# The later heads' exponentials stay in PSUM until their low halves are taken, and GpSimd makes the remainders of q and k in two column halves

## The chip, the cores and the metric

The kernel runs on one core of a Trainium2 chip. Five engines work side by side, each through its own queue in order: TensorE (PE; its weight loads are listed apart as PEld), VectorE (DVE), ScalarE (ACT), GpSimd (POOL) and SyncE (SP), which issues the transfers. The metric is the device time of one execution in microseconds. Before the change the median of three runs is 1068.91 us (1068.48 to 1070.02).

## The reference, cut to what matters

```python
# q, k, v: (8 batches, 8 heads, 576 rows, 64);  f: (8, 8, 576);  w_in: (512, 2048);  w_out: (2048, 512)
scores = q @ k.T / 8
cum    = cumsum(log(clip(f, 1e-4, 1)))
scores = where(causal, -1e9, scores + cum[:, None] - cum[None, :])
attn   = exp(scores - scores.max(-1))
attn   = attn / (attn.sum(-1) + 1e-9)
x      = (attn @ v), heads side by side              # 4608 x 512
h      = x @ w_in
g      = h * clip(h + 3, 0, 6) / 6
out    = g @ w_out
```

All of it is float32. Products on TensorE run on float16 pairs: a number is split into a high half (its cast to float16) and a low half (the number less its high half), and a product takes three matmuls (high by high, high by low, low by high). q and k are split likewise into a rounded part and a remainder.

## The kernel before, in words

Batch 0's heads run in another form: first two heads at a time for the first 256 rows (four steps "A", numbers 0 to 3), then each head for the rest (eight steps "B", 4 to 11). The other seven batches are the later batches: 56 steps "F", one for a head, numbers 12 to 67. A name such as `pn_40_1` is the tile `pn` of step 40, half 1.

A step F works in two halves. Half 0 holds the query chunks 1, 4 and 0 (192, 576 and 64 keys wide), half 1 the chunks 2 and 3 (320 and 448 wide), by `NAT`. For each half, in `rows`:

- PE makes the scores, row by row, into the two-bank PSUM tile `pn` (L611 from the rounded parts `TQ`, `TK`, L614 from the remainders in `T7`, `T1`). `pn` comes from the pool `ps_s`, which has two such tiles.
- DVE adds the causal mask `W`, copies the chunk into the SBUF tile `pp` and takes its row maximum (L622, followed by a small read of the accumulator). `pn` is then free for the next user. DVE makes the bias `nb` (L628).
- ACT takes the exponential in place in `pp` (L634) and casts it into the high half in a ring buffer `hl` (L648).
- The low halves are exponential less high half: the wide part of chunks 1 to 4 at L651, and the last 64 columns of two chunks in one instruction, 128 by 2 by 64, at L657 (the profile lists it as 128x128). Chunk 0's 64 columns are L662. `PL_POOL` and `B0_POOL` say which of these GpSimd does: in the eight heads of batch 1 (12 to 19) chunk 3's wide part, and in heads 20 to 67 all of L657 and L662. GpSimd zeroes a corner of `hl` first (L645).
- A transposing DMA turns `hl` into `pT`, from which PE makes the head's 40 matmuls of attention by v (`pav`, L694 to L699) one step later. DVE scales them (L730 to L732) and, after a head pair, splits them (ACT L737, DVE L738) for `xT`.

GpSimd rounds q and k (`parts`, L449 and L450) two steps ahead, and makes the remainders one step ahead (`rests`, L458 and L461, one instruction of 64 x 576 each).

The dense layers run in units between the attention's pieces. `h_unit` makes 128 columns of h for up to 512 rows (twelve matmuls, L777 to L779, into `ph`; ACT L783, DVE L786, ACT L787, DVE L788), and `out_unit` makes 128 rows of the output (48 matmuls, L824 to L826, into `po`; then ACT L830). `ph` and `po` rotate over three PSUM tiles once batch 0's first units are done. Before `out_unit` can run, `w_out` has to be scaled and split: ACT L284 makes a high half, DVE L295 the low half, sixteen pieces, all of them in the stretch around heads 12 to 18. A unit of a batch can only start when the batch's heads are done.

The order on each engine is not that of the code: the kernel is built with a scheduler that plays the program through its own model of time and writes each engine's queue accordingly. What a tile waits for, who holds it, and how long the planner takes an instruction to be, decide which row comes next.

Of the kernel before, what the change touches and what calls it, by code (L numbers as in the profile page):

```python
# [11 lines left out]
F32 = mybir.dt.float32  # L12
# [3 lines left out]
ALU = mybir.AluOpType  # L16
# [4 lines left out]
def kernel(  # L21
# [10 lines left out]
    nc = tc.nc  # L32

    NHEAD, D, S = qk.shape
# [5 lines left out]
    P = 128  # L40
# [13 lines left out]
    p2 = ctx.enter_context(tc.tile_pool(name="p2", bufs=2))  # L54
# [19 lines left out]
    W = cpool.tile([P, 4 * P + P], BF16, name="W")  # L74
# [23 lines left out]
    NV = len(VH)  # L98
    NRING = 3
    NSP = 3  # L100
    PL_POOL = ((3, ), ())
    NAT = ((1, 4, 0), (2, 3))
    B0_POOL = ((0, 0), (1, 1))
    W_AHEAD = (4, 5)
    W_ORDER = 0
    POOL_REST = ((0, 0, 0, 0), (0, 0, 0, 0))
# [1 line left out]
    TQ = [cpool.tile([97, SP], F32R, name=f"TQ{i}") for i in range(NQK)]  # L108
    TK = [cpool.tile([97, SP], F32R, name=f"TK{i}") for i in range(NQK)]
    T1 = [cpool.tile([P, SP], F32R, name=f"T1{i}") for i in range(NL)]  # L110
# [333 lines left out]
    def parts(v):  # L444
# [4 lines left out]
        nc.gpsimd.tensor_scalar(TK[i][0:D, 0:nk], s[D:, 0:nk], **one)  # L449
        nc.gpsimd.tensor_scalar(TQ[i][0:D, 0:nq], s[0:D, q0:q0 + nq], **one)  # L450

    def rests(v):
        i, j = v % NQK, v % NL
        s = ST[v % NST]
        nq, nk, q0 = spans(v)
        nc.sync.dma_start(T7[j].bitcast(F32)[0:D, 0:nq], TQ[i].bitcast(F32)[0:D, 0:nq])
        nc.sync.dma_start(T1[j].bitcast(F32)[D:, 0:nk], TK[i].bitcast(F32)[0:D, 0:nk])
        nc.gpsimd.tensor_tensor(  # L458
            T7[j][D:, 0:nq], s[0:D, q0:q0 + nq], TQ[i][0:D, 0:nq].bitcast(F32), op=ALU.subtract
        )  # L460
        nc.gpsimd.tensor_tensor(  # L461
            T1[j][0:D, 0:nk], s[D:, 0:nk], T1[j][D:, 0:nk].bitcast(F32), op=ALU.subtract
        )


    def chunks(v):
# [119 lines left out]
    o = 0  # L586
    for half in NAT:
        for c in half:
            HT[c] = o
            o += (2 * c + 1) * P  # L590
    PLACE = {1: 0, 4: 192, 0: 768, 3: 0, 2: 512}
    ringh = [t.bitcast(F16) for t in ring]

    def rows(v):
# [7 lines left out]
        for half in range(2):  # L602
            pn = ps_s.tile([P, 1024], F32, tag="S", name=f"pn_{v}_{half}")
            hl = ringh[(2 * v + half) % NRING]
            for c in NAT[half]:
# [3 lines left out]
                for a, e in zip(cut, cut[1:]):  # L609
# [4 lines left out]
                    nc.tensor.matmul(  # L614
                        dst, T7[j][:, qs], T1[j][:, a:e], start=False, stop=True
                    )
            pp = p2.tile([P, 832], F32, tag="Pp", name=f"pp_{v}_{half}")
            at, w = {}, 0
            for x, c in enumerate(NAT[half]):
                o, r, kw = PLACE[c], RR[c], RB[c] + RR[c]  # L620
                at[c] = w
                nc.vector.tensor_tensor_reduce(  # L622
                    pp[:r, w:w + kw], pn[:r, o:o + kw], W[:r, 4 * P + r - kw:4 * P + r],
                    1.0, -3.0e38, ALU.add, ALU.max, accum_out=mc[:r, e0 + x:e0 + x + 1],
                )
                w += kw
            e1 = e0 + len(NAT[half])
            nc.vector.tensor_scalar(  # L628
                nb[:, e0:e1], mc[:, e0:e1], -0.125, math.log(PSC), op0=ALU.mult, op1=ALU.add
# [435 lines left out]
```

## Time and profile before

| | |
|---|---|
| median of three runs | 1068.91 us |
| the profiled execution's own time | 1069.33 us |
| its span (first to last instruction of the trace) | 1067.5 us |
| mean granted TensorE clock | 0.988 |
| busy: PE, DVE, ACT, POOL | 1006.3, 731.1, 587.3, 403.4 us |

The span and the execution's time differ by 1.8 us, which no instruction of the trace covers. PE's busy time is the union of modelled durations: matmuls are pipelined, one of 512 columns is listed with 0.38 us while the next starts about 0.22 us behind it, so a matmul with nothing behind it still counts in full. Views by stretch matter here, since the stretches have different limits.

### The profile page before, as it was taken

What the parts mean: (1) busy time and instruction counts of PE and PEld (TensorE: products, weight loads), DVE (VectorE), ACT (ScalarE), POOL (GpSimd) and SP (SyncE); (2) the same over time, 40 slices, a digit from 0 to 9 for tenths busy, and PEclk for the clock granted to TensorE, in tenths of its full rate; (3) what the DMA queues carried; (4) which work ended last, traced back from release to release, by engine and by line L of the source; (5) the groups of instructions that cost most, each with busy time, mean ns of one, the idle gap of its engine ahead of it and who ended that gap; (6) DMA issues with size and microseconds to landing.
All of it is one profiled execution on the core that took longest, in us unless ns stands there. A gap on an engine that the chain in (4) does not pass through costs nothing.

```text
span 1067.5 us, 21157 instructions
## 1 busy us (share of the span) xinstructions
PE 1006.3 (94%) x7650; PEld 598.0 (56%) x7650; DVE 731.1 (68%) x1887; ACT 587.3 (55%) x1189; POOL 403.4 (38%) x505
## 2 busy tenths in 40 slices
PE   2799977899999999999999999999999999999897
PEld 1577844665555755555555755555555755444543
DVE  6978899996876768866886668846895677105300
ACT  4778666764764557545654557635764566115301
POOL 8343466443443444344443444534443330000000
PEclk9989989999999999999999999999999999999999
DMA  8965647955856776667575766566557554010000
GB/s 240 308 187 194 151 109 145 220 114 118 169 116 134 139 153 124 113 148 165 118 134 118 158 140 119 118 136 167 119 112 145 103 100 74 12 40 1 1 20 30
DMA packets 259155, 133.78 MB, mean 125 GB/s; under 512 B 226948, under 2 KB 228540, under 8 KB 259052
## 3 DMA queue, kind: packets, MB, share of 16 engines
q1 hardware_dynamic: 259052, 132.44, 55.7%
q8 instruction: 60, 0.98, 0.4%
q14 instruction: 43, 0.35, 0.1%
HBM read 47.93 MB, written 9.73 MB: 54 GB/s over the span
## 4 chain that ended last, share of the span: by engine, by line
PE 76%; DVE 12%; ACT 5%; issue 4%; DMA 2%; POOL 1%; SPq 0%; DVEq 0%; ACTq 0%; POOLq 0%
PE po L824 9%; PE po L826 9%; PE po L825 9%; PE ph L777 9%; PE ph L778 9%; PE ph L779 9%; PE pn L611 3%; PE pn L614 3%; DVE pp L622 2%; DVE ring L651 2%; PE po_r L826 1%; PE pav L698 1%; ACT pp L634 1%; PE po_r L824 1%; PE po_r L825 1%
## 5 line engine op out<-in xcount | busy, mean ns | idle before, releaser
L634 ACT ACTIVATE pp<-pp,nb 128x192 f32<-128x192 f32 x280 | 138.6, 552 | 170.3 <-DVE nb L628 150.8
L777 PE MATMUL ph<-xT,w 128*128 128x512 f16 (+1 forms) x576 | 198.8, 357 | 2.5 <-DVE r L786 2.4
L825 PE MATMUL po<-w,gT 128*128 128x512 f16 x512 | 192.6, 382 | 8.0 <-DVE w L295 8.0
L779 PE MATMUL ph<-xT,w 128*128 128x512 f16 (+1 forms) x576 | 198.0, 356 | 0.0
L778 PE MATMUL ph<-xT,w 128*128 128x512 f16 (+1 forms) x576 | 197.8, 356 | 0.0
L651 DVE TENSOR_TENSOR ring<-pp,ring 128x128 f16<-128x128 f32 (+2 forms) x216 | 138.0, 650 | 85.6 <-ACT ring L648 84.7
L824 PE MATMUL po<-w,gT 128*128 128x512 f16 x512 | 190.4, 383 | 5.8 <-DVE r_r L813 2.7
L826 PE MATMUL po<-w,gT 128*128 128x512 f16 x512 | 192.4, 383 | 0.0
L622 DVE CUSTOM_DVE_ANT_0 pp<-pn,W 128x192 f32<-128x192 f32 x280 | 123.3, 482 | 29.3 <-PE pn L614 28.0
L461 POOL TENSOR_TENSOR T<-ST,T 64x576 fp32r<-64x576 f32 (+1 forms) x68 | 100.9, 1483 | 107.2 <-DMA T<-TK 85.8
L786 DVE SCALAR_TENSOR_TENSOR r<-r,ph 128x512 f32<-128x512 f32 (+1 forms) x144 | 89.1, 620 | 61.4 <-ACT r L783 60.6
L611 PE MATMUL pn<-TK,TQ 68*128 68x192 f32 x336 | 124.8, 385 | 3.8 <-issue 2.2
L788 DVE TENSOR_TENSOR gT<-r,gT 128x512 f16<-128x512 f32 (+1 forms) x144 | 111.6, 781 | 22.0 <-ACT gT L787 20.6
L614 PE MATMUL pn<-T,T 128*128 128x192 f32 x336 | 115.2, 368 | 0.2 <-POOL T L461 0.2
L783 ACT ACTIVATE r<-ph,bias_r,SC 128x512 f32<-128x512 f32 (+1 forms) x144 | 103.9, 725 | 19.2 <-PE ph L779 17.1
L648 ACT CAST ring<-pp 128x192 f16<-128x192 f32 x280 | 114.2, 449 | 0.0
L787 ACT CAST gT<-r 128x512 f16<-128x512 f32 (+1 forms) x144 | 81.4, 567 | 59.6 <-DVE r L786 59.3
L449 POOL TENSOR_SCALAR TK<-ST 64x576 fp32r<-64x576 f32 (+1 forms) x68 | 49.2, 724 | 167.8 <-PE pn L611 142.9
L657 POOL TENSOR_TENSOR ring<-pp,ring 128x128 f16<-128x128 f32 x96 | 61.0, 636 | 116.1 <-ACT ring L648 75.2
L458 POOL TENSOR_TENSOR T<-ST,TQ 64x576 fp32r<-64x576 f32 (+2 forms) x68 | 95.2, 1400 | 17.7 <-PE pn L614 11.1
L826 PEld LDWEIGHTS <-gT 128*128 128x128 f16 x560 | 54.8, 98 | 74.5 <-issue 15.1
L825 PEld LDWEIGHTS <-gT 128*128 128x128 f16 x560 | 54.9, 98 | 66.5 <-issue 11.9
(158 smaller groups left out, 2010.2 us busy)
## 6 DMA issues: line engine op xcount, KB each, us to landing
ST<-in_qk_dram SPq DMA_DIRECT2D x64, 288.0 KB
T<-TK SPq DMA_DIRECT2D x64, 144.0 KB
ring<-in_w_out_dram SPq DMA_DIRECT2D x16, 512.0 KB
out_dram<-o SPq DMA_DIRECT2D x32, 256.0 KB
T<-TQ SPq DMA_DIRECT2D x56, 144.0 KB
vst<-in_vS_dram SPq DMA_DIRECT2D x7, 1040.0 KB
ring<-in_w_in_dram SPq DMA_DIRECT2D x9, 512.0 KB
w<-in_w_in_dram SPq DMA_DIRECT2D x7, 512.0 KB
```

Source lines behind the costliest of these rows:

```text
L611: nc.tensor.matmul(dst, TQ[i][0:D + 4, qs], TK[i][0:D + 4, a:e], start=True, stop=False)
L614: nc.tensor.matmul(dst, T7[j][:, qs], T1[j][:, a:e], start=False, stop=True)
L622: nc.vector.tensor_tensor_reduce(pp[:r, w:w + kw], pn[:r, o:o + kw], W[:r, 4 * P + r - kw:4 * P + r], 1.0, -3.0e38, ALU.add, ALU.max, accu ...
L634: nc.scalar.activation(x_, x_, AF.Exp, bias=nb[:r, e0 + x:e0 + x + 1], scale=0.125)
L648: nc.scalar.copy(hl[:r, h0[c]:h0[c] + kw], pp[:r, at[c]:at[c] + kw])
L651: eng.tensor_tensor(hl[:r, a:a + c * P], pp[:r, at[c] + 64:at[c] + kw], hl[:r, h0[c] + 64:h0[c] + kw], op=ALU.subtract,)
L777: nc.tensor.matmul(ph, w1[0][:, cc, fs_], xh, start=(cc == 0), stop=False)
L778: nc.tensor.matmul(ph, w1[0][:, cc, fs_], xl, start=False, stop=False)
L779: nc.tensor.matmul(ph, w1[1][:, cc, fs_], xh, start=False, stop=(cc == NCC - 1))
L824: nc.tensor.matmul(po, g[:, 0, fc, ts_], w2[:, fc, 0, :], start=(fc == 0), stop=False)
L825: nc.tensor.matmul(po, g[:, 0, fc, ts_], w2[:, fc, 1, :], start=False, stop=False)
L826: nc.tensor.matmul(po, g[:, 1, fc, ts_], w2[:, fc, 0, :], start=False, stop=(fc == NFC - 1))
```

## The change

The copy of the scores into `pp` is gone. DVE writes masked scores back into `pn`, ACT takes the exponential in place there and casts from there, and the low halves are read from there too. [...] The places of chunks 2 and 3 in `pn` are exchanged, so that the pair instruction steps forward from chunk 2 to chunk 3. `rests` makes each remainder in two instructions, 64 x 288 each for a full head (the helper is called `thirds`, but cuts in two).

```diff
-    PL_POOL = ((3, ), ())
+    PL_POOL = ((), ())
     NAT = ((1, 4, 0), (2, 3))
-    B0_POOL = ((0, 0), (1, 1))
+    B0_POOL = ((0, 0), (0, 0))
...
+    def thirds(n):
+
+        w = -(-n // 2)
+        return [(a, min(a + w, n)) for a in range(0, n, w)]
+
     def rests(v):
...
-        nc.gpsimd.tensor_tensor(
-            T7[j][D:, 0:nq], s[0:D, q0:q0 + nq], TQ[i][0:D, 0:nq].bitcast(F32), op=ALU.subtract
-        )
-        nc.gpsimd.tensor_tensor(
-            T1[j][0:D, 0:nk], s[D:, 0:nk], T1[j][D:, 0:nk].bitcast(F32), op=ALU.subtract
-        )
+        for a, e in thirds(nq):
+            nc.gpsimd.tensor_tensor(
+                T7[j][D:, a:e], s[0:D, q0 + a:q0 + e], TQ[i][0:D, a:e].bitcast(F32),
+                op=ALU.subtract,
+            )
+        for a, e in thirds(nk):
+            nc.gpsimd.tensor_tensor(
+                T1[j][0:D, a:e], s[D:, a:e], T1[j][D:, a:e].bitcast(F32), op=ALU.subtract
+            )
...
-    PLACE = {1: 0, 4: 192, 0: 768, 3: 0, 2: 512}
+    PLACE = {1: 0, 4: 192, 0: 768, 2: 0, 3: 512}
...
-            pp = p2.tile([P, 832], F32, tag="Pp", name=f"pp_{v}_{half}")
-            at, w = {}, 0
+            pp, at = pn, PLACE
             for x, c in enumerate(NAT[half]):
                 o, r, kw = PLACE[c], RR[c], RB[c] + RR[c]
-                at[c] = w
                 nc.vector.tensor_tensor_reduce(
-                    pp[:r, w:w + kw], pn[:r, o:o + kw], W[:r, 4 * P + r - kw:4 * P + r],
+                    pn[:r, o:o + kw], pn[:r, o:o + kw], W[:r, 4 * P + r - kw:4 * P + r],
                     1.0, -3.0e38, ALU.add, ALU.max, accum_out=mc[:r, e0 + x:e0 + x + 1],
                 )
-                w += kw
```

The lines below the change move down by five to eight: L611, L614, L622, L651, L657 and L662 of before are L619, L622, L628, L656, L662 and L667 of the changed kernel. The order of the queues moves too. Three places are shown.

The first is DVE's queue between heads 12 and 13, where the low halves of head 12 meet the splits of `w_out` (`w2`, L295). Before:

```order
L662 TENSOR_TENSOR ring0_123<-pp_12_0_1654,ring0_123 64x64
L295 SCALAR_TENSOR_TENSOR w2_115<-w2_115,SC_120 128x512
L622 ISA pp_13_0_1736,MF1_109<-pn_13_0_1727,W_88 128x192
L622 ISA MF1_109 128x1
L651 TENSOR_TENSOR ring1_124<-pp_12_1_1682,ring1_124 128x256
L622 ISA pp_13_0_1736,MF1_109<-pn_13_0_1727,W_88 128x576
```

And now:

```order
L295 SCALAR_TENSOR_TENSOR w2_115<-w2_115,SC_120 128x512
L656 TENSOR_TENSOR ring0_123<-pn_12_0_1671,ring0_123 128x128
L656 TENSOR_TENSOR ring1_124<-pn_12_1_1704,ring1_124 128x384
L662 TENSOR_TENSOR ring1_124<-pn_12_1_1704,ring1_124 128x2x64
L295 SCALAR_TENSOR_TENSOR w2_115<-w2_115,SC_120 128x512
L656 TENSOR_TENSOR ring0_123<-pn_12_0_1671,ring0_123 128x512
L628 ISA pn_13_0_1753,MF1_109<-pn_13_0_1753,W_88 128x192
```

Before, two of the sixteen splits stand ahead of head 13's first maximum, and the last four stand behind the low halves of head 16's half 0. Now seven stand ahead of it (two of them ahead of head 12), and the last stands within head 14, ahead of its low halves.

The second is PE's queue behind head 18's scores (`pav` is attention by v, `pT` a head's transposed halves). Before:

```order
L614 MATMUL pn_18_1_2572<-T10_99,T70_101 128x448
L824 LDWEIGHTS gT_116
L824 MATMUL po_0_0_1376<-w2_115,gT_116 128x512
L824 LDWEIGHTS gT_116
L824 MATMUL po_0_1_1511<-w2_115,gT_116 128x512
L694 LDWEIGHTS pT_16_2196
```

And now the place just ahead of head 19's scores:

```order
L702 MATMUL pav_110<-v16_111,pT_17_2380 128x65
L703 LDWEIGHTS pT_17_2380
L703 MATMUL pav_110<-v16_111,pT_17_2380 128x64
L704 LDWEIGHTS pT_17_2380
L704 MATMUL pav_110<-v16_111,pT_17_2380 128x65
L619 MATMUL pn_19_0_2684<-TK1_97,TQ1_94 128x192
L622 MATMUL pn_19_0_2684<-T11_100,T71_102 128x192
```

Between the scores of heads 18 and 19 PE now has only the 40 matmuls of `pav`; between those of 19 and 20 these and six of `ph_1`. Before, the output units `po_0_0` and `po_0_1` lie spread over heads 13 to 19, and fifteen units of h for batch 0's second half of rows between heads 19 and 20. Now `po_0_0` starts ahead of head 12, and all of these lie between heads 12 and 17.

The third is ACT's queue in head 40, a head of the later stretch, with what each row waits for. Before:

```order
L648 CAST ring2_125<-pp_40_0_6350 128x192 [waits DMAHW4_49,Activation_49]
L783 ACTIVATE r_3_6_0_6370<-ph_3_6_0_6329,bias_r_86,SC_120 128x512 [waits PE_49]
L648 CAST ring2_125<-pp_40_0_6350 128x576 [waits Activation_49]
L648 CAST ring2_125<-pp_40_0_6350 64x64 [waits Activation_49]
L783 ACTIVATE r_3_7_0_6397<-ph_3_7_0_6375,bias_r_86,SC_120 128x512 [waits PE_49]
```

And now:

```order
L653 CAST ring2_125<-pn_40_0_6367 128x192 [waits DMAHW4_49,Activation_49]
L653 CAST ring0_123<-pn_40_1_6429 128x320 [waits DMAHW7_49,Activation_49]
L792 CAST gT_116<-r_3_8_0_6453 128x512 [waits DVE_49]
L788 ACTIVATE r_3_9_0_6477<-ph_3_9_0_6464,bias_r_86,SC_120 128x512 [waits PE_49]
L653 CAST ring2_125<-pn_40_0_6367 128x576 [waits DVE_49]
L653 CAST ring0_123<-pn_40_1_6429 128x448 [waits DVE_49]
L792 CAST gT_116<-r_3_9_0_6477 128x512 [waits DVE_49]
L653 CAST ring2_125<-pn_40_0_6367 64x64 [waits DVE_49]
```

The second and third cast of a half now wait for DVE, which has to finish the low half of the chunk before. The next head's first score matmul in turn waits for the last low half that reads the tile.

## The prediction

> **What bounds the kernel now.** I cut the span into stretches first, by where the heads and the dense work change.
>
> ```profile
> 0.00:132.00 132.00, 101.80 (x654) 80.97 (x654) 107.17 (x298) 89.97 (x186) 65.39 (x85) 0.96 0.73 216
> 132.00:199.00 67.00, 51.43 (x438) 32.77 (x437) 65.35 (x183) 43.05 (x91) 42.83 (x39) 0.90 0.66 146
> 199.00:250.00 51.00, 48.22 (x421) 33.51 (x419) 40.04 (x114) 29.87 (x70) 16.28 (x20) 1.00 0.69 140
> 250.00:900.00 650.00, 648.24 (x5243) 373.63 (x5242) 482.35 (x1239) 383.36 (x779) 278.93 (x363) 1.00 0.64 131
> ```
>
> The columns behind the length are the busy times of PE, PEld, DVE, ACT and POOL, the granted clock, and the transfers. From 250 to 900 us PE is busy 648.2 of 650.0 us, at full clock. From 132 to 199, the first seven heads of the later form, DVE is busy 65.4 of 67.0 us and PE only 51.4. Next I asked what PE waits for, first from 132 to 250 us, then from 250 to 900.
>
> ```profile
> PE po L825 <- DVE w L295: 8.0, 4, 3.8
> PE pav L694 <- DMA pT<-ring: 4.3, 5, 2.2
> ```
>
> ```profile
> PE po L824 <- DVE e_v L187: 0.9, 1, 0.9
> PE ph L777 <- DVE r L786: 0.7, 1, 0.7
> PE ph_r L800 <- DVE r_r L813: 0.2, 1, 0.2
> ```
>
> So from 250 us on there are 1.8 us to be won, whatever the change does to DVE, ACT and POOL. The stretch before is another matter: the chain of waits from 132 to 199 us runs over DVE's copies, low halves and splits.
>
> ```profile
> by line: DVE pp L622 16.2%; DVE ring L651 14.2%; DVE ring L657 12.3%; DVE w L295 10.9%; issue 10.6%; DVE v L400 8.4%; ACT pp L634 3.8%; DVE xhl L738 3.7%; DVE ring L662 3.0%; ACT w L284 2.1%; PE pn L611 1.9%; DVE xf L732 1.7%; DVE nb L628 1
> ```
>
> That is where I look for the gain. A loss can come from anywhere.
>
> **DVE's instructions, priced.** The groups of DVE from 132 to 199 us, then the group of L786 from 250 to 900:
>
> ```profile
> L657 DVE TENSOR_TENSOR ring<-pp,ring 128x128 f16<-128x128 f32 x11 | 9.0, 817 | 0.0
> ...
> L622 DVE CUSTOM_DVE_ANT_0 pp<-pn,W 128x576 f32<-128x576 f32 x7 | 5.2, 746 | 0.0
> L651 DVE TENSOR_TENSOR ring<-pp,ring 128x512 f16<-128x512 f32 x6 | 4.7, 784 | 0.3 <-ACT ring L648 0.3
> L651 DVE TENSOR_TENSOR ring<-pp,ring 128x256 f16<-128x256 f32 x6 | 4.7, 778 | 0.0
> ...
> L622 DVE CUSTOM_DVE_ANT_0 pp<-pn,W 128x320 f32<-128x320 f32 x6 | 2.9, 475 | 0.1
> ...
> L662 DVE TENSOR_TENSOR ring<-pp,ring 64x64 f16<-64x64 f32 x6 | 2.5, 410 | 0.0
> ...
> L622 DVE CUSTOM_DVE_ANT_0 pp<-pn,W 64x64 f32<-64x64 f32 x7 | 1.5, 209 | 0.0
> ```
>
> ```profile
> L786 DVE SCALAR_TENSOR_TENSOR r<-r,ph 128x512 f32<-128x512 f32 x91 | 61.6, 678 | 5.8 <-ACT r L783 5.4
> ```
>
> L657 is 128 wide and takes longer than a 512-wide instruction should need. The timelines of DVE (first three rows) and POOL (last row) show why:
>
> ```profile
> 758.29 0.69 DVE L788 TENSOR_TENSOR gT<-r,gT 128x512 f16<-128x512 f32 x1
> ...
> 759.57 1.48 DVE L651 TENSOR_TENSOR ring<-pp,ring 128x384 f16<-128x384 f32 x1
> 760.97 0.92 DVE L788 TENSOR_TENSOR gT<-r,gT 128x512 f16<-128x512 f32 x1
> ```
>
> ```profile
> 759.22 1.41 POOL L461 TENSOR_TENSOR T<-ST,T 64x576 fp32r<-64x576 f32 x1 [2.23 <-DMA T<-TK]
> ```
>
> L651 starts at 759.57 behind GpSimd's instruction, which ends at 760.63, and ends 0.42 us behind that: it was held for its length. Both inputs of L651 lie in SBUF; L786 and L622 have one in PSUM. The low halves will also have one in PSUM. I price them by L622: 209 ns at 64 columns, 475 at 320, 746 at 576, so 1.05 ns a column and 142 ns, which gives 276 at 128, 411 at 256, 545 at 384, 680 at 512 (L786 has 678). Saved in the stretch: 11 x (817 - 276) + 6 x (784 - 680) + 6 x (778 - 411) + 6 x (410 - 209) ns = 10.0 us. Added: six of chunk 3's wide part from GpSimd, 6 x 545 = 3.3 us. The maxima of a half now wait for one another, three times a head; such a wait costs what lies between these rows:
>
> ```profile
> 761.88 0.67 DVE L786 SCALAR_TENSOR_TENSOR r<-r,ph 128x512 f32<-128x512 f32 x1
> 762.48 0.18 DVE L731 RECIPROCAL rs<-rs 128x5 f32<-128x5 f32 x1
> 762.69 0.49 DVE L732 TENSOR_TENSOR xf<-pav,rs 128x320 f32<-128x320 f32 x1
> ```
>
> L731 starts 0.07 us ahead of L786's end, L732, which waits for L731, 0.03 us behind: 0.1 us, so 2 us for seven heads. DVE gains some 4.7 us of its 65.4 (bounds: 0, if writes into PSUM, which no row shows, cost 0.1 us each; 8, if the splits and L400 are held less too).
>
> [...]
>
> From 250 to 900 us DVE takes over L657 and L662, some 47 x (2 x 276 + 209) ns = 36 us, and loses the holds on L651. It has 482.4 of 650.0 us busy, and PE covers it.
>
> **The queues' new order** matters more. PE's work between head 12 and the end of `po_0_3` follows from the order and from PE's steps (two timelines):
>
> ```profile
> 248.09 0.19 PE L699 MATMUL pav<-v,pT 128*128 128x65 f16 x1
> ...
> 248.90 0.38 PE L824 MATMUL po<-w,gT 128*128 128x512 f16 x1
> ...
> 249.97 0.38 PE L826 MATMUL po<-w,gT 128*128 128x512 f16 x1
> 250.00 0.44 PE L611 MATMUL pn<-TK,TQ 68*128 68x192 f32 x1
> ```
>
> ```profile
> 132.01 0.35 PE L611 MATMUL pn<-TK,TQ 68*128 68x192 f32 x1
> ```
>
> 26 of `pav` take 0.81 us, 0.031 each; five steps of `po` 1.07, 0.214 each. Four output units are 192 x 0.214 = 41 us, sixteen half-wide units of h 192 x 0.107 = 21, nine heads' scores about 2.1 each (twice 1,600 columns at 0.214/512 us, and some 0.8 for weight loads that are not hidden, an allowance) = 19, nine times 40 of `pav` 11: 92 us, done now between 132.0 and 250.0. So PE stands without a new matmul for 26 us, more than the busy times say, since a lone matmul's tail counts as busy.
>
> The change does this work, and eighteen matmuls of `ph_1` more (3.9 us), with the splits of `w_out` done by head 14. They end at 195 now:
>
> ```profile
> L295 DVE SCALAR_TENSOR_TENSOR w<-w,SC x16: 732/736/1966, 144.3 to 195.0; 128x512 f16<-128x512 f32 x16
> ```
>
> Its time is 92 + 3.9 = 96 us of work, and three sums of waiting. At the start, PE now issues `po_0_0` ahead of head 12 and so waits for the first split: 4 us (0 to 7; the split stood 12 us behind head 12's start, most of it head 12's own rows and the v splits). In heads 12 to 16 DVE's splits and the releases of `pn`: 4 us, half of today's 8.0 for L295, as DVE's 4.7 us go to the splits (2 to 12; 12 is half of today's 26). In heads 18 and 19 PE has 2.1 + 40 x 0.031 = 3.3 us of work, and 4.6 with six of `ph_1`, while the tile comes free only when the last low half is taken. That chain by its rows (ACT's from 250 to 900 us):
>
> ```profile
> L634 ACT ACTIVATE pp<-pp,nb 128x576 f32<-128x576 f32 x47 | 35.7, 760 | 0.0
> L648 ACT CAST ring<-pp 128x576 f16<-128x576 f32 x47 | 31.2, 664 | 0.0
> ```
>
> For half 0 (832 columns in three chunks) DVE's maxima 1.3 us, ACT's exponentials about 1.5, its casts 1.25, the low halves with pair and corner 1.45, the bias 0.15: 5.7 us in a row, and 7.5 with half 1's share on the same engines. So 4 us and 3 us late, and with the transposes behind them 9 together (5 to 13). The sum: 96 + 4 + 4 + 9 = 113, so 132 + 113 = 245, where today's kernel has the same work done at 250 + 3.9 = 253.9: 9 us gained.
>
> **What is given back.** The halves of `rests` cost GpSimd. From the whole span's groups:
>
> ```profile
> L458 POOL TENSOR_TENSOR T<-ST,TQ 64x576 fp32r<-64x576 f32 x56 | 82.5, 1473 | 15.3 <-PE pn L614 11.1
> ...
> L458 POOL TENSOR_TENSOR T<-ST,TQ 64x320 fp32r<-64x320 f32 x8 | 7.6, 948 | 0.6
> ```
>
> 2.05 ns a column and 292 ns each, so two halves 1.76 us for 1.47. GpSimd's total still falls, as it loses the low halves. Before 132 us, where the first scores wait for it, I allow 1 us. In the 48 heads behind 250 us, `pn` is held until the low halves are done. There PE has 11 to 13 us from a tile's last matmul to its next use, against 7.5, stretched by what stands between on DVE and ACT; I take 1 us in all (0 to 20). Net 9 - 1 - 1 = 7 us off the profiled execution's 1069.3, so 1062.3; the median of the runs lies 0.4 lower: 1062.
>
> **The rivals.**
> *Slower: the held tile stalls PE in every dense head.* In heads with six units of h, such as head 40, 25 rows stand on DVE between the first maximum and the last low half, some 14 us of durations and 12 with their overlaps; from the score's last matmul to the next use PE has about 12. If PE waits 0.5 us in each of 48 heads, 24 us go, 9 come back, with the 1 of the start 1085; it decides from 0.2 us a head. For it: the casts now wait for DVE twice a half, and both queues are in order. Against: DVE has a quarter of its time free. If half the heads do it, 1072. [...] 0.23.
> *No difference: the work of the first stretch is only shifted.* PE finishes the early units sooner, then waits 16 us instead of 9 in heads 17 to 20: 1069. For it: batch 1's dense work cannot start until head 19 is done, whatever was done before. 0.15.
> *A larger gain.* DVE is held less by GpSimd's shorter instructions, the first split costs 1 us instead of 4 and the late heads 4 instead of 9: 1054. 0.14.
> The forecast has 0.48.
>
> **The numbers.** 1062; on its own 1057 to 1067. The range takes in the larger gain and half of the slow rival: 1052 to 1075. Runs of this kernel tell 0.2%, 2.1 us, from no change. Faster: 0.47 of the forecast and the larger gain, 0.61; the same 0.15; slower 0.24.
>
> **What would show it.** L295's last instance near 160 us; the new low halves at 276 and 680 ns without instances of 1.4 us; PE's waits with DVE behind `pn` (L619), some 4 us long, around heads 18 and 19, and in sum under 3 us behind head 21. Wrong would be: such waits in most heads up to 900 us; low halves dearer by 0.1 us or more; or head 12's scores later than 140 us.

## The result, and the profile after

| | before | after |
|---|---|---|
| median | 1068.7 us (1068.29 to 1070.02) | 1076.64 us (1074.74 to 1077.62) |
| ratio | | 1.0058, 95% interval 1.0036 to 1.0081 |
| span of the profiled execution | 1067.5 us | 1075.6 us |
| first score of head 12, of head 21 | 132.0, 250.0 us | 137.2, 261.3 us |
| busy: DVE, POOL | 731.1, 403.4 us | 710.0, 342.3 us |

The change is slower by 0.58% where 0.6% faster was forecast. The cut into stretches, in the columns that the prediction explains:

```profile
132.00:199.00 67.00, 60.93 (x490) 42.96 (x490) 57.97 (x173) 43.36 (x94) 27.70 (x36) 0.95 0.62 129
199.00:250.00 51.00, 38.39 (x332) 26.45 (x331) 33.82 (x113) 24.21 (x58) 22.08 (x33) 0.81 0.69 143
...
300.00:900.00 600.00, 599.66 (x4874) 348.87 (x4872) 436.68 (x1274) 345.42 (x711) 208.26 (x294) 1.00 0.65 133
```

From 132 to 199 us DVE fell from 65.4 to 58.0 us and PE rose from 51.4 to 60.9: the work that the prediction saw moving forward did move. That window holds seven heads before and little over four now, so DVE's sums are better compared from head 12's first score to head 21's (before, then after):

```profile
132.01:250.00 117.99, 99.64 (x855) 66.28 (x855) 105.38 (x296) 72.92 (x161) 59.10 (x58) 0.94 0.68 144
137.18:261.35 124.17, 105.50 (x859) 70.58 (x857) 95.02 (x299) 69.52 (x157) 49.29 (x67) 0.89 0.66 137
```

DVE's busy time did fall by 10 us over these nine heads, and they took 6 us longer. From 199 to 250 PE fell from 48.2 to 38.4, and its granted clock from 1.00 to 0.81. From 300 to 900 us it stood 0.34 us. So nearly all of the loss lies ahead of 300 us.

DVE's groups from 250 to 900 us, by shape, show that the new low halves, all of them DVE's by the emptied tables, have their forecast price (683 ns for 680, 281 and 283 for 276) and that none is held beside GpSimd's work any more: of L656, L662 and L667 the longest took 692 ns, where 43 of the 216 rows of L651 took over 900 ns before, up to 1764, each of them beside a GpSimd instruction. The splits of `w_out` (last row) end at 175 instead of 195:

```profile
L656 DVE TENSOR_TENSOR ring<-pn,ring 128x512 f16<-128x512 f32 x47 | 32.1, 683 | 8.5 <-ACT ring L653 8.4
L662 DVE TENSOR_TENSOR ring<-pn,ring 128x128 f16<-128x128 f32 x94 | 26.2, 281 | 4.7 <-ACT ring L653 4.7
L656 DVE TENSOR_TENSOR ring<-pn,ring 128x128 f16<-128x128 f32 x47 | 13.3, 283 | 15.0 <-ACT ring L653 11.4 <-DMA T<-TK 3.6
```

```profile
L295 DVE SCALAR_TENSOR_TENSOR w<-w,SC x16: 730/736/899, 134.6 to 175.0; 128x512 f16<-128x512 f32 x16
```

What PE waits for from 137 to 300 us (total, times, longest):

```profile
PE pav L699 <- DMA pT<-ring: 12.1, 9, 5.7
PE po L830 <- DVE w L295: 2.1, 2, 1.9
PE pn L619 <- ACT xhl L742: 1.8, 1, 1.8
```

The waits for the low halves of `w_out` fell from 8.0 to 2.1 us, as forecast; one of 1.2 us for a high half (ACT, L284) came. In their place PE waits 12.1 us for a head's transposed halves. PE's timeline shows where, from head 18's scores to those of head 20:

```profile
221.75 0.44 PE L619 MATMUL pn<-TK,TQ 68*128 68x192 f32 x1
...
223.46 0.37 PE L622 MATMUL pn<-T,T 128*128 128x448 f32 x1
229.49 0.23 PE L699 MATMUL pav<-v,pT 128*128 128x65 f16 x1 [5.66 <-DMA pT<-ring]
...
233.64 0.50 PE L619 MATMUL pn<-TK,TQ 68*128 68x192 f32 x1 [1.79 <-ACT xhl L742]
...
239.91 0.24 PE L699 MATMUL pav<-v,pT 128*128 128x65 f16 x1 [2.94 <-DMA pT<-ring]
...
242.33 0.59 PE L782 MATMUL ph<-xT,w 128*128 128x512 f16 x1
242.71 0.63 PE L783 MATMUL ph<-xT,w 128*128 128x512 f16 x1
...
244.44 0.44 PE L619 MATMUL pn<-TK,TQ 68*128 68x192 f32 x1
```

What the first of these waits ends on is seen in the timelines of DVE and SP (two rows; SPq is SP's sequencer, which issues):

```profile
222.53 0.20 DVE L667 TENSOR_TENSOR ring<-pn,ring 64x64 f16<-64x64 f32 x1
222.56 4.47 SPq L674 DMA_TRANSPOSE pT<-ring  x2
```

Head 17's last low half is done at 222.73, before PE begins to wait. From there its two transposing DMAs, issued one behind the other by SP, take until 229.49: 6.8 us. For head 18 it is 4.7 us (235.19 to 239.91).

With no dense work left, the two heads take 11.9 and 10.8 us, and PE does 3.3 and 4.6 us of work in them. The rows at 242 show a second loss: two dense matmuls stand 0.38 us apart, against 0.214 in the prediction's rows. PE's clock is down there. The same stretch, cut where the granted clock changes:

```profile
222.00:227.30 5.30, 1.83 (x13) 1.43 (x11) 3.36 (x15) 1.52 (x4) 2.90 (x4) 1.00 0.93 199
227.30:244.40 17.10, 10.11 (x97) 7.88 (x98) 11.19 (x32) 7.37 (x18) 4.86 (x8) 0.50 0.67 138
244.40:247.80 3.40, 1.92 (x20) 1.69 (x18) 3.34 (x13) 0.53 (x1) 1.75 (x3) 1.00 0.87 165
247.80:251.20 3.40, 3.40 (x12) 1.66 (x10) 2.17 (x13) 2.67 (x6) 2.26 (x4) 0.50 0.88 173
```

Within the wait of 5.66 us, at 227.3, the clock falls; it is at half for 17.1 us, and again for 3.4. From the spacing of the matmuls in these windows (`pav` 0.054 us for 0.031, scores 3.1 us a head for 1.9, dense steps 0.43 for 0.215) that costs 5.8 us, beside some 12 us of waits.

### The profile page after: what moved, and what is told of

The parts are those of the page before. It is cut to its first block, busy times and chain, and to the rows that moved or that the text cites. A ratio compares the mean times of both kernels' runs of the same rounds, so it can differ in the third digit from the quotient of the medians.

```text
span 1075.6 us, 21009 instructions
## 1 busy us (share of the span) xinstructions
PE 1012.8 (94%) x7650; PEld 604.6 (56%) x7650; DVE 710.0 (66%) x2039; ACT 582.2 (54%) x1189; POOL 342.3 (32%) x489
## 4 chain that ended last, share of the span: by engine, by line
PE 75%; DVE 9%; DMA 6%; ACT 4%; issue 3%; POOL 3%; SPq 0%; POOLq 0%; ACTq 0%; DVEq 0%
PE po L830 10%; PE po L831 10%; PE po L829 10%; PE ph L782 8%; PE ph L784 8%; PE ph L783 8%; PE pn L619 3%; PE pn L622 3%; DMA pT<-ring 3%; DMA ring<-in_w_out_dram 2%; PE pav L703 1%; PE pav L704 1%; PE pav L702 1%; PE ph_r L805 1%; PE ph_r L807 1%
## 5 line engine op out<-in xcount | busy, mean ns | idle before, releaser
L639 ACT ACTIVATE pn<-pn,nb 128x192 f32<-128x192 f32 (+1 forms) x280 | 134.1, 498 | 144.9 <-DVE nb L633 142.2
L628 DVE CUSTOM_DVE_ANT_0 pn<-pn,W 128x192 f32<-128x192 f32 x280 | 136.2, 498 | 44.0 <-PE pn L622 40.1
L469 POOL TENSOR_TENSOR T<-ST,T 64x288 fp32r<-64x288 f32 (+1 forms) x136 | 114.1, 858 | 124.2 <-DMA T<-TK 123.3
L464 POOL TENSOR_TENSOR T<-ST,TQ 64x288 fp32r<-64x288 f32 (+2 forms) x136 | 110.7, 815 | 122.0 <-PE pn L622 98.2
L656 DVE TENSOR_TENSOR ring<-pn,ring 128x128 f16<-128x128 f32 (+1 forms) x224 | 106.3, 482 | 54.5 <-ACT ring L653 50.7
L653 ACT CAST ring<-pn 128x192 f16<-128x192 f32 (+1 forms) x280 | 112.3, 425 | 35.8 <-DVE ring L656 32.9
L788 ACT ACTIVATE r<-ph,bias_r,SC 128x512 f32<-128x512 f32 (+1 forms) x144 | 105.0, 730 | 35.9 <-PE ph L784 34.6
L619 PE MATMUL pn<-TK,TQ 68*128 68x192 f32 x336 | 120.8, 378 | 2.0 <-ACT xhl L742 1.8
L793 DVE TENSOR_TENSOR gT<-r,gT 128x512 f16<-128x512 f32 (+1 forms) x144 | 95.6, 668 | 27.4 <-ACT gT L792 26.1
L622 PE MATMUL pn<-T,T 128*128 128x192 f32 x336 | 108.3, 348 | 0.0
L650 POOL MEMSET ring<- 64x128 f16 x56 | 11.2, 201 | 278.3 <-DMA pT<-ring 267.2
L831 PEld LDWEIGHTS <-gT 128*128 128x128 f16 x560 | 54.9, 98 | 67.9 <-issue 8.2
L830 PEld LDWEIGHTS <-gT 128*128 128x128 f16 x560 | 54.9, 98 | 64.6 <-issue 8.3
L829 PEld LDWEIGHTS <-gT 128*128 128x128 f16 x560 | 54.2, 98 | 60.6 <-issue 8.4
```

The lines of the kernel that those rows point to most:

```text
L469: nc.gpsimd.tensor_tensor(T1[j][0:D, a:e], s[D:, a:e], T1[j][D:, a:e].bitcast(F32), op=ALU.subtract)
L619: nc.tensor.matmul(dst, TQ[i][0:D + 4, qs], TK[i][0:D + 4, a:e], start=True, stop=False)
L622: nc.tensor.matmul(dst, T7[j][:, qs], T1[j][:, a:e], start=False, stop=True)
L628: nc.vector.tensor_tensor_reduce(pn[:r, o:o + kw], pn[:r, o:o + kw], W[:r, 4 * P + r - kw:4 * P + r], 1.0, -3.0e38, ALU.add, ALU.max, accu ...
L639: nc.scalar.activation(x_, x_, AF.Exp, bias=nb[:r, e0 + x:e0 + x + 1], scale=0.125)
L653: nc.scalar.copy(hl[:r, h0[c]:h0[c] + kw], pp[:r, at[c]:at[c] + kw])
```

## The experiments

The theory after the result: the held tile lengthens every head's way from its scores to its transposed halves, dense work moves ahead into the longer heads, the last heads of batch 1 stand bare, and the clock falls there. Rivals: the halves of `rests`, through the later start of head 12; the 48 later heads; chance, since the planner's order changes with any edit. Each ratio below is against the kernel before, with its 95% interval. The rounds ran on different chips, on which the kernel before took 1068.7 to 1072.3 us at the median, so ratios are compared and not medians.

### Which part, and in which heads

"Halves only" is the diff of `rests` alone; "PSUM only" is the rest of the diff. The other two choose by head, with halves, and give GpSimd its share of the low halves back in the heads that copy. (`n` counts heads from batch 0 on: step 12 has n = 8, which is `H`; `v` is the step's number.)

```diff
-            pp, at = pn, PLACE
+            keep = n >= 2 * H          # PSUM late; n < 2 * H: PSUM first
+            if keep:
+                pp, at = pn, PLACE
+            else:
+                pp = p2.tile([P, 832], F32, tag="Pp", name=f"pp_{v}_{half}")
...
```

Halves only:

> Only the remainders are made in two halves; exponentials, low halves and GpSimd's tables are as before. The change is 7.7 us slower by its median, and head 12 starts 5.2 us later in it (137.2 against 132.0 us). Theory A (two causes in series): the halves reorder the queues ahead of head 12, where `po_0_0` now stands, and so delay head 12 by about 5 us; the held tiles of heads 12 to 19 cost the rest. Then head 12 starts near 137 us here, DVE's surplus in heads 13 to 16 hides part of it, and the kernel takes about 1072 us (1070 to 1074). Theory B (the held tiles alone, the start is hidden anyway): 1069, within 0.2% of before. Theory C (any edit shuffles the planner's order by such amounts): no relation, anything from 1065 to 1077, and head 12's start not tied to the halves.

PSUM only:

> The changed kernel with the remainders whole again. Theory A: head 12 starts near 132 us as before, heads 18 to 20 wait for their transposed halves as in the change, the dense work of batch 0 lies early, and the kernel takes about 1073 us (1071 to 1075). Theory B: as the change, 1076 to 1077. If the halves are the whole loss, 1066 to 1069.

PSUM late (heads 20 to 67):

> The change with one part undone: in heads 12 to 19 the exponentials lie in SBUF as before, chunk 3's low half on GpSimd; from head 20 on they stay in PSUM; the remainders are in halves. Theory A: the stretch of heads 12 to 19 is as with the halves alone, and the later heads cost nothing, since PE is busy 599.66 of 600 us there in the change: the time of the kernel with halves alone, about 1072, within 1.5 us. A rival that puts the loss on the later heads (48 times a little): about 1076.

PSUM first (heads 12 to 19):

> The other half: exponentials in PSUM in heads 12 to 19 alone, later heads as before with GpSimd's low halves, remainders in halves. Theory A: heads 12 to 20 as in the change, and so its time, 1076 to 1077. The rival that puts the loss on the later heads: 1072 or less.

| | median, us | ratio |
|---|---|---|
| halves only | 1070.54 | 1.0002 (0.998 to 1.0024) |
| PSUM only | 1078.60 | 1.0079 (1.0052 to 1.0107) |
| PSUM late, halves | 1073.61 | 1.0018 (0.9995 to 1.004) |
| PSUM first, halves | 1077.47 | 1.0058 (1.0036 to 1.0081) |

The loss comes with the exponentials in PSUM in heads 12 to 19. With them it is whole (the last row equals the change), without them it is within the error, though the intervals of the last two rows touch. By these times theory A, which gave half of the loss to the halves, fell. One profile of each kernel shows where its time goes (us, the last column from head 12's first score to head 67's):

| | head 12 starts | heads 12 to 66 |
|---|---|---|
| before | 132.0 | 753.4 |
| halves only | 132.5 | 749.7 |
| PSUM only | 132.1 | 759.6 |
| PSUM late, halves | 138.0 | 753.1 |
| PSUM first, halves | 140.2 | 753.7 |
| the change | 137.2 | 756.3 |

Behind head 12's start the PSUM form costs 6.2 us with whole remainders and 6.6 with halves, and the halves win some 3.5. In the change 5.2 us more are lost ahead of that start, where the clock falls a second time at 70.3 us. Ten of the eleven profiles with halves in batch 0 show a second fall at 70 to 74 us, halves only is the exception, and none of the nine others shows one there (from 60 to 90 us the clock was 0.89 in the change and in PSUM late, 0.88 in PSUM first, 1.00 in halves only and PSUM only, 0.98 before). So the halves may cost some 4 us at the start and win about as much behind it. From one profile each this is an estimate, and too coarse to divide the loss by heads: behind the start PSUM late costs 3.4 us over halves only, and PSUM first 4.0.

To ask the same of the later heads without halves, and with the casts ahead of the low halves (explained below), one more kernel kept the PSUM form to heads 20 on:

> Exponentials in SBUF in heads 12 to 19 as before, in PSUM from head 20 on with the casts first, remainders whole everywhere: the change without the two parts to which the loss is traced. If the later heads cost nothing and win nothing, 1070 to 1072, within 0.2% of before; if PSUM in the later heads costs the 2 us by which the kernel with halves and late PSUM stood above the one with halves alone, 1073.

1072.16 us, 1.0015 (0.9991 to 1.0039). So the later heads win nothing, and whether they cost up to 4 us these runs cannot tell.

### The bare heads

Dense matmuls of batch 1 were held back to their heads:

```diff
+                    sm = nc.tensor.matmul(
                         dst, T7[j][:, qs], T1[j][:, a:e], start=False, stop=True
                     )
+                    anchor[0] = sm.ins if H <= n < PACED else None
...
+            behind = tc.issue_after(anchor[0]) if anchor[0] else nullcontext()
-            with tc.high_priority(offset=-LOW_M):
+            with behind, tc.high_priority(offset=-LOW_M):
                 r = next(units[0], 0)
```

> The change, and with it one rule for the order: in batch 1 (heads 12 to 19) a dense matmul that the program emits during head v may not be queued ahead of head v's half-0 scores. The same dense work is done by head 20, but evenly: 8.2, 9.8, 9.0, 9.0, 5.1, 6.4, 7.7, 9.0 and 11.6 us in heads 12 to 20, where the change has 9.1, 10.6, 7.3, 12.2, 13.9, 7.3, 1.2, 2.5, 11.6. Theory D (the loss is the bare heads 18 and 19, whose chain has nothing to hide behind, and the clock that falls there): the 12 us of waits there shrink to 3 to 5 and the half clock to at most one window; about 1064 us (1060 to 1069). Theory H (a held tile slows each of the eight heads, wherever the dense work lies): 1073 to 1077, as the change.

1076.63 us, 1.0051 (1.0028 to 1.0073): theory D's number failed, and theory H's came. Heads 18 and 19 lost their waits, but heads 12 to 16 still took 10.8 to 16.6 us, and head 21, with 10.3 us of dense work and `pav`, 17.3. By head 21's start this profile was 6.7 us ahead of the change's, with the same work done; it lost 3.2 of them in head 21, which took 14.1 us in the change, and 2.7 behind head 67's first score. (Here and in the expectations the dense work of a head includes its 40 matmuls of `pav`, 1.2 us.)

The same was tried from the other end, with more of the dense work given out early (`F_RATE` 0.6 for 0.45), on the kernel with whole remainders and the casts ahead:

> Exponentials in PSUM, casts first, whole remainders (1074.2 at a rate of 0.45), and the program gives out the dense units of batch 1 at a rate of 0.6. Dense work in heads 12 to 20: 5.3, 7.2, 7.3, 6.8, 9.8, 10.3, 17.4, 8.5, 6.9 us, 79.5 us by head 20 instead of 77.5. If what counts is how much dense work stands beside the held heads, 2 to 4 us less, 1070 to 1072; if heads 12 to 15 decide, whose work is the same, 1074.

1075.86 us, 1.0052 (1.0033 to 1.0071), against 1.0014 without it. Its stretches:

```profile
199.00:250.00 51.00, 50.62 (x447) 34.26 (x446) 39.45 (x123) 28.41 (x68) 18.54 (x20) 1.00 0.66 134
250.00:300.00 50.00, 41.98 (x299) 23.66 (x300) 42.09 (x119) 31.72 (x67) 17.46 (x20) 0.86 0.76 152
```

PE is busy 50.6 of 51 us up to 250, and then has 8 us of the next 50 without work, with the clock at 0.86: the bare place has moved to head 21, whose dense work cannot start before batch 1's last heads are done. Dense work that is done earlier is missed later.

The third trial filled the wait with matmuls that nobody reads:

```diff
+            if v in FILL:                     # FILL = {17: 36, 18: 18}
+                with tc.issue_after(anchor[0]):
+                    for _ in range(FILL[v]):
+                        nc.tensor.matmul(
+                            pav[:, 0:NCH, 0:D], w1[0][:, 0, 0:P],
+                            w1[0][:, 0, 0:NCH * D].rearrange("p (c d) -> p c d", c=NCH),
+                            start=True, stop=True,
+                        )
```

> The change, with 54 idle matmuls of 320 columns (36 behind head 18's scores, 18 behind head 19's) that write into the attention tile and are overwritten: about 7 us of added work in which PE would otherwise wait for the transposed halves. Theory K (the waits let TensorE's clock fall to half for 17 us, which makes the scores, the attention and the first dense matmuls behind them some 5.8 us longer): the granted clock stays at 1.00 from 227 to 244 us, and the kernel takes 1072 to 1074. Theory W (the waits alone decide, the slower matmuls lie inside them): 1076 to 1078; more, if the added matmuls delay the attention.

1074.19 us, 1.0033 (1.0013 to 1.0053). Its windows:

```profile
219.00:227.00 8.00, 8.00 (x55) 5.51 (x52) 4.74 (x17) 2.84 (x7) 2.91 (x4) 1.00 1.04 176
227.00:237.80 10.80, 7.34 (x111) 5.89 (x111) 9.27 (x28) 4.70 (x11) 5.31 (x8) 1.00 0.70 146
237.80:251.50 13.70, 12.19 (x41) 6.56 (x41) 11.07 (x39) 7.15 (x18) 6.75 (x9) 0.50 0.68 137
```

The clock stays at 1.00 ten us longer and then falls all the same. Some 7 us of added work (54 x 320/512 x 0.215), and the ratio is 0.25% below the change's. The two intervals overlap; the direction is that of theory K, its full size was not reached.

### The ring, and the old form in the bare heads

ACT's cast of head 18 waits for a ring buffer until the transposing DMA has read it (ACT's timeline of the change):

```profile
229.52 0.65 ACT L653 CAST ring<-pn 128x320 f16<-128x320 f32 x2 [1.40 <-DMA pT<-ring]
```

```diff
-    NRING = 3
+    NRING = 4
```

(two early tiles of the decay share another tag, which makes the room.)

> The change with four ring buffers for the halves' fp16 pairs instead of three (the room is what the copy `pp` took; two early tiles of the decay get another place). PE's order is that of the change. In the change ACT's first cast of head 18 waits 1.4 us for the transposing DMA that still reads its ring buffer, and that DMA ends together with the one PE waits for. Theory T (the ring's three buffers and the DMA behind them set the time of a bare head): heads 18 and 19 take 9 to 10 us instead of 11.9 and 10.8, half a clock window less, the kernel 1071 to 1074. Theory C (the ring is one wait among several in a chain that runs from the scores over DVE, ACT, DVE, and the transposing DMA to the attention): 1075 to 1077.

1076.43 us, 1.0042 (1.0023 to 1.0061): theory C. The cast's wait is gone, PE's is not:

```profile
PE pav L699 <- DMA pT<-ring: 10.9, 6, 4.7
```

Together with the pacing, at a rate of 0.5:

> Four ring buffers, and the dense matmuls of batch 1 held back to their heads (8.2, 9.8, 9.0, 10.3, 6.4, 7.7, 6.4, 11.6, 8.4 us in heads 12 to 20). Theory T: the pacing, which alone left the time at 1076.6 because heads of some 12 us stood around 8 us of dense work, now has shorter heads to fill: 1066 to 1071. Theory C: 1073 to 1077, as the pacing alone.

1090.05 us, 1.018 (1.0151 to 1.0208), outside both expectations. PE waits 11.6 us for transposed halves behind 300 us, where the change has 0.3 us of such waits. Which of its three edits brings these waits was not tried apart (the rate of 0.6, in the other form above, brings none); nothing follows on the ring from it.

With the old form from head 18 on (`keep = n < 14`):

> Exponentials in PSUM only in heads 12 to 17; heads 18 and on as before (GpSimd's low halves in heads 20 on), remainders in halves. Dense work lies as in the change up to head 17; heads 18 to 20 are bare of it (0.0, 1.2 and 2.5 us), but their tiles come free right behind the maxima. Theory H (the held tile sets the time of a bare head): they take 8 us or less instead of 11 to 12, and the kernel about 1070 us. Theory T (the ring of three buffers and its transposing DMA set it): a bare head takes 10 to 12 us in this form too, and the kernel 1075 to 1080.

1077.43 us, 1.0065 (1.0041 to 1.0088). Heads 18 to 20 took 2.5, 10.7 and 8.2 us, 7.1 on the mean, as theory H had it, though head 19 alone took 10.7 with PE idle for 7.1 of them; and heads 21 to 23 gave the gain back (head 23 took 11.7 us with 3.2 us of `pav` and dense work). Theory T's time came out for another reason than the one given.

### What makes a held head long

The hold alone, added to the kernel before:

```diff
+            if n < 2 * H:
+                keep = p2.tile([P, 2], F32, tag="kp", name=f"kp_{v}_{half}")
+                lo = NAT[half][1]
+                k = GH[half][lo] + lo * P
+                nc.vector.tensor_tensor(
+                    keep[:, 0:1], pn[:, 0:1], hl[:, k - 64:k - 62].bitcast(F32), op=ALU.subtract,
+                )
...
```

> Before, plus the hold alone: in heads 12 to 19 two tiny DVE instructions a half read the scores' tile behind the last low half, so that it comes free as late as in the change; exponentials, low halves and GpSimd's work stay as they were. The order alone shows that the hold moves dense work forward: 5.3, 9.3, 9.0, 6.4, 9.0, 9.6, 10.7, 6.6 us in heads 12 to 19, against 2.4, 3.7, 5.1, 4.7, 4.3, 5.1, 4.7, 21.8. Theory D: no row of bare heads (head 20 alone has 0.3 us), so no loss: 1062 to 1070. Theory H: 1074 to 1078.

1072.46 us, 1.0015 (0.9996 to 1.0034). The hold moves dense work forward, but costs 4 us at the most. So the PSUM form, 1.0079 with whole remainders as here, costs more than its hold. What else differs is seen in the order of ACT that was shown of head 40: the casts and the low halves now read one PSUM tile in turns, each waiting for the other engine. One loop cut in two takes the turns away:

```diff
             for c in NAT[half]:
                 r, kw, a = RR[c], RB[c] + RR[c], GH[half][c]
                 nc.scalar.copy(hl[:r, h0[c]:h0[c] + kw], pp[:r, at[c]:at[c] + kw])
+            for c in NAT[half]:
+                r, kw, a = RR[c], RB[c] + RR[c], GH[half][c]
                 if c:
```

With halves, and with whole remainders:

> The change, with one loop cut in two: all casts of a half are emitted ahead of its low halves. In the change the casts and the low halves read the same PSUM tile in turns, and each turn is a wait: in a head three casts wait for DVE and five of DVE's low halves for ACT, each behind what else stands in the other's queue. With the casts first no cast waits for DVE, and two low halves wait for ACT. Theory P (the turns between ACT and DVE are what lengthens a held head; holding the tile alone left the time at 1072.5): heads 12 to 19 shorten from 13.4 us to some 12, waits in 140 to 300 us fall by 5 or more, the kernel 1068 to 1072. Theory B (a held head is long because its steps follow each other anyway): the sum of the steps is the same, 1075 to 1077.

> The same with the remainders whole (the change with whole remainders took 1078.6). Dense work in heads 12 to 20 then lies at 5.3, 7.2, 7.3, 6.8, 9.8, 10.3, 13.3, 6.0 and 11.6 us, the most even of all so far, with no bare head. Theory P: 1066 to 1071, below the kernel before if anything is. Theory B: 1076 to 1079.

| | in turns | casts first |
|---|---|---|
| whole remainders | 1078.60, 1.0079 (1.0052 to 1.0107) | 1074.21, 1.0014 (0.9995 to 1.0032) |
| halves (the change) | 1076.64, 1.0058 (1.0036 to 1.0081) | 1077.19, 1.0047 (1.0026 to 1.0068) |

ACT's casts from 132 to 250 us (idle time before them at the end of the row), whole remainders in turns, then casts first:

```profile
L645 ACT CAST ring<-pn 128x192 f16<-128x192 f32 (+4 forms) x40 | 15.7, 424 | 6.0 <-DVE ring L648 5.9
```

```profile
L645 ACT CAST ring<-pn 128x192 f16<-128x192 f32 (+4 forms) x45 | 15.8, 437 | 0.1
```

With whole remainders the edit wins 0.65%, and the intervals lie apart. It also moves dense work: in turns, heads 12 to 20 hold some 7, 9, 9, 9, 11, 13, 5, 2.5 and 12 us, against the row that was expected above, so not all of the gain need be the turns. With halves, as in the change itself, the same edit won nothing: there ACT's casts no longer wait for DVE either (8.4 us in the same window in the change), but 3.7 us for the transposing DMA. Two more kernels asked whether the halves ahead of head 12 stand between (`SPLIT` is whether a remainder is cut):

```diff
+        SPLIT[0] = v >= 20            # late; v < 12: early
```

> Exponentials in PSUM, casts first, remainders in halves only from head 20 on. Queues up to head 20 are those of the kernel with casts first and whole remainders (1074.2). Theory S (the halves cost at the start: head 12 began at 136.8 to 140.2 us in nine of ten profiles with halves, at 131.0 to 132.1 in three of four without): head 12 starts near 132 and the kernel takes 1074 us. Theory L (halves cost in the later heads, or casts first helps only by chance): 1077.

> The complement: remainders in halves only in batch 0 (steps 0 to 11), whole from head 12 on, exponentials in PSUM, casts first. Queues up to head 20 are those of the kernel with casts first and halves (1077.2). Theory S: head 12 starts near 137, the dense work of heads 12 to 20 shifts with it, 1077. Theory L: 1074.

Late: 1072.52 us, 1.0017 (1.0002 to 1.0033). Early: 1082.04 us, 1.0098 (1.0076 to 1.0121). Theory S's sign is right: halves in batch 0 cost, halves in the later heads do not. Its size is not: early halves alone cost 5 us more than halves everywhere (1.0047), though PE's dense work lies alike up to head 20. That difference stays open, and why the halves cost nothing without the PSUM form has only the estimate above.

Last, on the kernel with casts first and whole remainders (1.0014), DVE's work was taken away where it was thought to be the bound:

```diff
-    POOL_REST = ((0, 0, 0, 0), (0, 0, 0, 0))
+    POOL_REST = ((0, 0, 0, 0), (0, 1, 0, 1))     # all splits: (1, 1, 1, 1)
```

> Exponentials in PSUM, casts first, whole remainders, and eight of the sixteen splits of `w_out` taken from DVE: ACT scales the piece in place and GpSimd, which has nothing to do with low halves any more, subtracts. If DVE's work bounds heads 12 to 15 (it was busy throughout there, and PE waited 17 us in those four heads with casts first and whole remainders), eight times 0.74 us go from its path: 1068 to 1071, below the kernel before. If the steps of a head bound it, 1074 or, with more of the dense work left for heads 20 and 21, 1072 to 1076.

> The same with all sixteen splits on ACT and GpSimd. DVE loses 11.8 us, GpSimd takes some 16 times 1.2 us, ACT 16 times 0.7 us. DVE theory: 1064 to 1070. Steps theory: 1074 to 1080, since heads 12 to 19 then hold only some 4 to 5 us of dense work each and the rest, 32 us, lies in head 21.

1080.68 us, 1.009 (1.0064 to 1.0115), and 1089.80 us, 1.0179 (1.0152 to 1.0206): less work on DVE, and slower. The first stretch with eight and with sixteen splits moved:

```profile
132.00:199.00 67.00, 49.29 (x376) 30.89 (x374) 51.11 (x166) 41.94 (x87) 35.68 (x36) 0.87 0.64 140
```

```profile
132.00:199.00 67.00, 48.78 (x395) 32.66 (x394) 49.55 (x160) 44.88 (x93) 39.98 (x42) 0.87 0.65 145
```

No engine is busy for more than 51.1 of the 67 us. With eight moved, PE waits 11.5 us for transposed halves from 140 to 300 us, 6.6 for the splits that DVE still makes and 1.5 for GpSimd's; with all sixteen, 10.8 us for these, which take 1,177 ns each, so that the second kernel does not speak for a head's steps alone. In the first, heads 13 to 17 take 11.6 us on the mean with 5.3 us of dense work and `pav` in each; before, with 4.6, they took 10.1. This speaks for a head's steps in a row as the bound, not DVE's sum; which step it is was not tried.

No version beat the kernel before.

## Why the prediction was wrong

Its sum was 4 us at the start, 96 of work, 4 of waits in heads 12 to 16 and 9 in heads 18 and 19: 245. Head 21 started at 261.3. With the prediction's own steps (dense matmuls from the order at 0.215 us, 0.031 for `pav`, 2.1 for a head's scores) the 16 us go like this, where a head's time is from its first score matmul to the next head's:

| step | predicted | measured |
|---|---|---|
| start of head 12 | 4 | 5.2 |
| work, heads 12 to 20 | 96 | 94.6 |
| heads 12 to 16, time less work | 4 | 75.6 - 63.6 = 12.0 |
| head 17 | 0 | 8.9 - 9.4 = -0.5 |
| heads 18 to 20, time less work | 9 | 39.6 - 21.6 = 18.0 |

**Priced rightly.** The new low halves, the direction of DVE's surplus (10 us over nine heads, where 4.7 were forecast for seven), the forward move of the dense work, the end of the splits' waits, no stall in the 47 heads behind. The writes into PSUM, which the sum put at nothing, cost some 0.07 us each, inside the bound of 0.1 that it gave. A low half with a PSUM source took 683 ns at 512 columns; an unheld row of DVE without one took 0.69 us before (L788 at 758.29, 512 columns). The 0.8 us that a head's scores have for weight loads in the sum was an allowance; the scores of head 18, twelve matmuls at full clock, took 1.9 us by their spacing, for 2.1 with it.

**The step that failed** is the last: "that chain by its rows". Its 9 us were waits at full clock. Measured are some 12 us of waits in heads 18 to 20, and 5.8 us by the half clock, which begins in the first of them. The sum had 4 and 3 us for the chain up to the last low half, which left 2 for the transposes of two heads; from the last low half to the first `pav` they took 6.8 and 4.7 us, and PE's two long waits lie wholly inside these. The chain was also summed as busy time in a row, 5.7 and 7.5 us a head; the turns between ACT and DVE, whose removal won 0.65% with whole remainders and nothing with halves, were put among the points for a rival in dense heads and left out of the sum here.

**Heads 12 to 16** were undersized by 8: 6.7 us without a matmul (3.3 of them for `w_out`'s halves), 6.8 us at half clock with PE busy 5.6 of them (some 3 us), and batch 0's `pav` in head 12, float32 and 2.9 us long, which the steps price at 0.4. This last fault is in the sum for before too.

**Against the kernel before** the trace reads like this: head 21 starts 11.3 us later; 5.2 of these stand at head 12's start already, and 3.9 are work of `ph_1` done ahead. Between the first scores of heads 12 and 21 PE has no matmul for 18.7 us, before for 18.4, and the clock is at half for 27.3 us, before for 13.7. The waits that were to shrink only moved, to a place with nothing beside them. The prediction put the 26 us that PE loses here in the kernel before down to waits and a lone matmul's tail; they are 18.4 us without a matmul, some 4.5 of clock (PE is busy 9.0 of the 13.7 us at half) and 2.5 of that float32 `pav`. The half clock, 0.90 in its own first rows, has no term in the sum.

**The start** came out by size, and by luck, for another reason than the one given. No wait for a split of `w_out` stands ahead of head 12. It begins late because batch 0's steps do, and in this profile the clock fell a second time in them, at 70.3 us for 6.8. Two kernels with the same PE queue up to there, halves only and PSUM late, from 60 to 90 us:

```profile
60.00:90.00 30.00, 28.12 (x183) 20.76 (x182) 24.50 (x80) 24.64 (x51) 14.22 (x21) 1.00 0.76 222
```

```profile
60.00:90.00 30.00, 27.11 (x156) 19.39 (x155) 21.71 (x68) 21.75 (x45) 13.57 (x20) 0.89 0.67 202
```

Their head 12 started at 132.5 and 138.0 us. Over all profiles with halves in batch 0 it was 132.5 to 140.2, over those without 130.8 to 135.8. So a start differs by some 5 us between two profiles with one PE queue, and the halves, for which the prediction allowed 1 us, shift its mean by about 4.

**The rivals.** "The work of the first stretch is only shifted" was the nearest. Its mechanism is what the kernel with the higher rate shows, and 16 us of waits in heads 17 to 20 was its number, against 17.5 measured of time less work (some 12 of waits, the rest the clock). It ended at 1069 since it kept the other sums. The rival on the other side, a stall in every dense head, is wrong: PE is busy 599.66 of 600 us.

**What stays open**: which part of a held head's added time is the hold, which the turns and which the planner's new order when all are there with halves (every edit moves the queues, and kernels that compute the same lay between 1.0002 and 1.018), and whether the PSUM form costs up to 0.4% in the later heads.

## What to carry to other kernels

Where an engine looks full, ask whether the stretch ends when its work is done or when a chain of steps is; here DVE lost 10 of 105 us in heads 12 to 20 and, with eight splits moved, 13, and these heads took longer, 124 and 126 us for 118. Work that another stage needs as cover is not won by doing it sooner: follow it to the place where it will be missed. Two engines that read one tile in turns waited for each other here (from 132 to 250 us ACT's casts waited 5.9 us for DVE with whole remainders, 8.4 in the change); letting one finish first is worth a trial, which won 0.65% in one form and nothing in the other.

## What the runs showed of the hardware

In the two profiles, before and after, TensorE's granted clock changed, up to 1000 us, only at distances of 3.41 us and multiples of it (at half for 3.41, 6.83, 10.24 and 17.07 us). From 100 to 1000 us it fell to 0.50 five times, and this is how long PE was busy in the 3.41 us ahead of each fall:

| profile | the 3.41 us ahead of the fall | PE busy, us |
|---|---|---|
| before | 139.95 to 143.36 | 1.45 |
| before | 177.50 to 180.91 | 1.23 |
| after | 148.81 to 152.22 | 1.53 |
| after | 223.91 to 227.32 | 0.00 |
| after | 244.39 to 247.80 | 1.93 |

So it fell behind partly busy steps too: in the last one the longest gap was 1.1 us. Busy time alone does not tell which steps: before, 163.84 to 167.25 and 235.52 to 238.93 had 1.58 and 1.75 us, and the clock stayed at 1.00 behind both. It came back behind steps with 2.85 us busy (before, 150.19 to 153.60) and 3.35 us or more (the other four times); behind one with 2.82 (after, 234.14 to 237.56) it stayed at half.

With DVE's masked scores in PSUM, the read of the accumulator behind a maximum took 140 ns, against 81 before (250 to 900 us, 128 rows), and the maximum itself 10 to 17 ns more (766 for 752 at 576 columns, 361 for 351 at 192, 228 for 211 at 64). ACT's rows were shorter: in the same window the exponential of 576 columns took 714 ns in PSUM and 760 in SBUF, the cast 641 and 664.
